# Residual stream in token-major layout, transposes by DMA crossbar, output weights resident: one core's attention and feed-forward block

## The chip, the cores and the metric

One core of a Trainium2 chip runs the whole program. The metric is device time in microseconds (us); a lower number is better. Runs of one kernel below agree within about 0.5%. All timed runs below are on one core, and each was interleaved with runs of the kernel before on the same chip. The experiments ran in three batches, each on another chip, and the kernel after did not run again beside them; the median of the kernel before moved by only 0.4 us between the batches (1413.09 to 1413.52), so times are compared across them, but differences of a few us are only good to about 2 us. "PE" is TensorE's matmul row in the profile, "PEld" its weight loads, "DVE" is VectorE, "ACT" is ScalarE, "POOL" is GpSimd and "SP" is SyncE, which here issues every DMA.

## The reference

An adaptive-layernorm block over 2048 tokens of width 1024: grouped-query attention over a cached window of 512 keys (32 query heads, 4 key heads, head size 128), then a gated feed-forward of width 3584. Cut to what matters:

```python
mod = (silu(c) @ w_mod).reshape(...)            # six rows of 1024: sa ca ga sb cb gb
h = layernorm(x) * (1 + ca) + sa
q = h @ wq                                      # 1024 -> 32 x 128
p = softmax(q @ k_window.T * 128 ** -0.5)       # 512 keys
x = x + ga * ((p @ v_window) @ wo)              # 4096 -> 1024
h = layernorm(x) * (1 + cb) + sb
x = x + gb * ((silu(h @ w_gate) * (h @ w_up)) @ w_down)
```

## The kernel before

Both kernels go through the tokens in four chunks of 512, first attention and output projection for all chunks, then the feed-forward for all chunks. A small tracker emits the instructions in program order and adds semaphore waits. Each engine's queue, and SP's queue of DMA issues, runs in order.

The kernel before keeps the residual feature-major (`xT`: feature on the partition, token along the free axis). So a layernorm sum runs over partitions and is a matmul with a matrix of ones; x has to be transposed on the way in and the result on the way out:

```python
def ln_task(...):                       # one chunk, dealt out as background steps
    for dt in range(DT):                # squares on GpSimd
        T.op(POOL, lambda: g.tensor_tensor(ln_sq[dt], xT[:, dt, chs], xT[:, dt, chs], ALU.mult), ...)
    for dt in range(DT):                # sums on TensorE
        mm(bank(bS), ones_bf, xT[:, dt, chs], ...)
    ...
    for dt in range(DT):
        mm(bank(bS), ones_bf, ln_sq[dt], ...)
    ...                                 # Ln and Exp on ScalarE for 1/sqrt, then three passes on VectorE
```

Per head, the attention output comes token-major out of the product with V, is normalised by VectorE, transposed by TensorE and copied out of PSUM:

```python
def otr(i):
    for j in range(TPC):
        transpose(bb[:, j * P:(j + 1) * P], o_s[os_][:, j, :], [B_os[os_]], PB[TRB])
    T.op(DVE, lambda: V.tensor_copy(oT_all[:, h, :], bb[:, 0:CH]), writes=[PB[TRB], B_oT[h]])

for i in range(NA + 3):                 # one turn per head; NA = 4 chunks x 32 heads
    if h % 4 == 2 and ...: load_wq(ch, h // 4 + 1)      # 1 MB of query weights
    if h == 8:  load_wo(0)                              # 2 MB of output weights, again in each chunk
    if h == 12: load_wo(1)
    ...
    qproj(i); scores(i - 1); pv(i - 2); otr(i - 3)
    ...                                 # after the last head of a chunk: oproj_plain(chunk)
```

The softmax here doesn't subtract the row's maximum and nothing guards it: scores larger than these inputs give would overflow.

## Time and profile before

The time is 1413.49 us (median of 3 runs, 1412.7 to 1415.42). The first lines come from the page of the kernel before: the span, the busy time of PE with its share and instruction count, the clock granted to TensorE in 40 slices of the span (9 is 90% or more), and the shares of the chain that ended last.

```profile
span 1412.8 us, 20538 instructions
PE 1346.9 (95%) x8445; PEld 700.7 (50%) x8592; DVE 610.2 (43%) x1324; ACT 415.0 (29%) x674; POOL 59.4 (4%) x65
...
PEclk7999999999999999999999999999999999999999
...
PE 91%; DVE 3%; issue 2%; ACT 2%; SPq 2%; DMA 1%; DVEq 0%; ACTq 0%
```

TensorE is the bound: it is busy 95% of the span, at nearly its full clock. What can be removed from it is in the groups of PE instructions by form (busy us, mean ns of one, idle time just before and its cause):

```profile
L289 PE MATMUL ps<-ident,arena 128*128 128x128 bf16 x528 | 51.0, 221 | 1.4 <-DVE arena L637 1.4
L285 PE MATMUL ps<-xT,ones_bf 128*128 128x512 bf16 x62 | 16.3, 410 | 4.0 <-DVE arena L637 3.0 <-DVE xT L355 0.9
L285 PE MATMUL ps<-ln_sq,ones_bf 128*128 128x512 bf16 x60 | 14.4, 379 | 4.2 <-DVE arena L637 3.2 <-DVE ln_mean L432 0.9
...
L289 PE MATMUL ps<-ident,xT 128*128 128x128 bf16 x128 | 10.5, 220 | 4.3 <-DVE xT L776 2.9 <-DVE xnat L789 1.4
```

The first line is the transposes of the attention output (512, and 16 of the keys), the next two are the layernorm sums, the last is the transposes of the result. A steady head in the timeline (start us, duration us, what) shows the pace:

```profile
326.70 0.38 PE L289 MATMUL ps<-ident,arena 128*128 128x128 bf16 x4
...
327.14 1.67 PE L285 MATMUL ps<-hT,arena 128*128 128x512 bf16 x7
...
328.65 1.96 PE L285 MATMUL ps<-arena 128*128 128x512 bf16 x20
...
330.45 0.38 PE L289 MATMUL ps<-ident,arena 128*128 128x128 bf16 x4
```

From one group of four transposes to the next it is 330.45 - 326.70 = 3.75 us. The durations overlap (327.14 + 1.67 lies after 328.65), because the profile models the ends of matmuls; so the pace is read from the starts.

### The profile page before, as it was taken

Reading aid. Unit: us, or ns where it says so; the run is one execution under the profiler, and the core shown is the slowest. Engines: PE = TensorE matmul, PEld = TensorE weight load, DVE = VectorE, ACT = ScalarE, POOL = GpSimd, SP = SyncE. Lnnn points to the kernel's source line nnn. Section 1 sums busy time; section 2 is a strip of 40 time slices with the busy share of each in tenths; the row PEclk is TensorE's granted clock in tenths of the full one; section 3 lists DMA queues with packets and bytes.
Section 4 is the critical chain, followed back from the end, with each engine's and each line's share of the span. In section 5 each row is a group of like instructions: output and inputs, shape, how many; then the busy total and the mean of one; then the engine's idle time right before and its main releaser. Section 6 shows DMA issues by size and latency. Waiting matters only on the chain.

```text
span 1412.8 us, 20538 instructions
## 1 busy us (share of the span) xinstructions
PE 1346.9 (95%) x8445; PEld 700.7 (50%) x8592; DVE 610.2 (43%) x1324; ACT 415.0 (29%) x674; POOL 59.4 (4%) x65
## 2 busy tenths in 40 slices
PE   5989999999999999999999999999999999999998
PEld 3556644556545566455554444444443444444443
DVE  4566554656613566235671245313331333124311
ACT  4455540456503666025760021001110111001100
POOL 0220021000010000110001100000000000000000
PEclk7999999999999999999999999999999999999999
DMA  9663204522143421434204485308721683129410
GB/s 304 199 183 120 90 31 120 154 86 61 61 120 111 120 69 61 117 92 121 75 16 114 141 268 171 111 15 271 222 96 52 200 278 126 52 94 300 151 52 30
DMA packets 237357, 178.53 MB, mean 126 GB/s; under 512 B 7888, under 2 KB 233168, under 8 KB 237264
## 3 DMA queue, kind: packets, MB, share of 16 engines
q1 hardware_dynamic: 237264, 177.22, 41.0%
q8 instruction: 67, 1.10, 0.3%
q14 instruction: 26, 0.21, 0.1%
HBM read 173.02 MB, written 4.19 MB: 125 GB/s over the span
## 4 chain that ended last, share of the span: by engine, by line
PE 91%; DVE 3%; issue 2%; ACT 2%; SPq 2%; DMA 1%; DVEq 0%; ACTq 0%
PE ps L285 89%; PE ps L289 2%; ACT arena L603 1%; DVE xT L776 1%; DMA xnat<-in_A_x_dram 1%; DVE arena L626 1%; DVE rl L623 1%; SPq L526 0%; SPq L361 0%; ACT L603 0%; ACT L447 0%; DVE xnat L789 0%; SPq L530 0%; DVE ln_var L440 0%; DVE arena L628 0%
## 5 line engine op out<-in xcount | busy, mean ns | idle before, releaser
L285 PE MATMUL ps<-arena 128*128 128x512 bf16 (+1 forms) x4431 | 671.0, 306 | 17.4 <-DVE xT L776 11.0
L285 PE MATMUL ps<-hT,arena 128*128 128x512 bf16 x2724 | 618.6, 380 | 16.0 <-ACT hT L466 6.4
L285 PEld LDWEIGHTS ps<-arena 128*128 128x128 bf16 x4480 | 365.8, 98 | 339.3 <-issue 15.3
L285 PEld LDWEIGHTS ps<-hT,arena 128*128 128x128 bf16 x2816 | 270.5, 98 | 318.5 <-DMA arena<-in_A_wq_dram 6.3
L603 ACT ACTIVATE arena<-ps 128x512 bf16<-128x512 f32 x512 | 305.5, 597 | 347.0 <-PE ps L285 312.2
L756 ACT ACTIVATE arena<-ps 128x512 bf16<-128x512 f32 x112 | 66.9, 597 | 543.7 <-PE ps L285 543.7
L757 DVE SCALAR_TENSOR_TENSOR arena<-arena,ps 128x512 bf16<-128x512 bf16 x112 | 77.0, 688 | 173.5 <-ACT arena L756 173.5
L591 DVE CAST arena<-ps 128x512 bf16<-128x512 f32 x128 | 88.4, 690 | 49.8 <-PE ps L285 45.1
L776 DVE SCALAR_TENSOR_TENSOR xT<-ps,c,xT 128x512 bf16<-128x512 f32 x32 | 22.6, 747 | 183.2 <-PE ps L285 183.2
L760 DVE SCALAR_TENSOR_TENSOR arena<-arena,ps 128x512 bf16<-128x512 bf16 x112 | 77.0, 688 | 53.8 <-PE ps L285 53.7
L651 DVE SCALAR_TENSOR_TENSOR xT<-ps,c,xT 128x512 bf16<-128x512 f32 x32 | 24.0, 751 | 152.3 <-PE ps L285 152.1
L427 POOL TENSOR_TENSOR ln_sq<-xT 128x512 bf16<-128x512 bf16 x56 | 58.4, 1060 | 717.3 <-PE ps L285 671.8
L626 DVE TENSOR_TENSOR arena<-ps,rl 128x384 bf16<-128x384 f32 x128 | 71.4, 558 | 4.4
L622 DVE RECIPROCAL rl<-ps 128x3 f32<-128x3 f32 x128 | 23.1, 180 | 110.7 <-PE ps L285 110.7
L637 DVE COPY arena<-ps 128x512 bf16<-128x512 bf16 x128 | 53.1, 415 | 0.2 <-PE ps L289 0.2
L289 PE MATMUL ps<-ident,arena 128*128 128x128 bf16 x528 | 51.0, 221 | 1.4 <-DVE arena L637 1.4
L628 DVE TENSOR_SCALAR arena<-ps,rl 128x128 bf16<-128x128 f32 x128 | 44.9, 351 | 4.6
L289 PEld LDWEIGHTS ps<-ident,arena 128*128 128x128 bf16 x528 | 35.7, 98 | 1.6 <-DVE arena L637 1.6
L462 DVE TENSOR_TENSOR ln_n<-ln_t,ln_B 128x512 bf16<-128x512 bf16 x64 | 28.4, 444 | 1.2
L459 DVE TENSOR_TENSOR ln_t<-xT,ln_A 128x512 bf16<-128x512 bf16 x64 | 27.5, 430 | 0.0
L623 DVE RECIPROCAL rl<-ps 128x1 f32<-128x1 f32 x128 | 21.5, 168 | 13.6 <-PE ps L289 0.5
L285 PE MATMUL ps<-xT,ones_bf 128*128 128x512 bf16 x62 | 16.3, 410 | 4.0 <-DVE arena L637 3.0
(48 smaller groups left out, 207.6 us busy)
## 6 DMA issues: line engine op xcount, KB each, us to landing
arena<-in_A_wq_dram SPq DMA_DIRECT2D x32, 1024.0 KB, 5.4
arena<-in_A_wo_dram SPq DMA_DIRECT2D x16, 2048.0 KB, 10.7
arena<-in_B_w_gate_dram SPq DMA_DIRECT2D x28, 1024.0 KB, 5.2
arena<-in_B_w_up_dram SPq DMA_DIRECT2D x28, 1024.0 KB, 7.2
arena<-in_B_w_down_dram SPq DMA_DIRECT2D x16, 1792.0 KB, 11.8
hT<-in_w_mod_dram SPq DMA_DIRECT2D x8, 1024.0 KB, 9.4
xnat<-in_A_x_dram SPq DMA_DIRECT2D x16, 256.0 KB, 5.6
arena<-in_w_mod_dram SPq DMA_DIRECT2D x4, 1024.0 KB, 10.2
```

Of the source, the lines that this page charges most:

```text
L285: T.op(PE, lambda: TE.matmul(out_ap, lhsT, rhs, start=start, stop=stop), reads=reads, writes=[bank_buf])
L289: T.op(PE, lambda: TE.transpose(out_ap, in_ap, ident[:, :]), reads=reads + [B_ident], writes=[bank_buf])
L427: T.op(POOL, lambda: g.tensor_tensor(ln_sq[dt][:, :], xT[:, dt, chs], xT[:, dt, chs], ALU.mult), reads=[B_xT[dt][ch]], writes=[B_sq[dt]])
L591: T.op(DVE, lambda: V.tensor_copy(qT_s[qs], bank(QB)), writes=[PB[QB], B_qT[qs]])
L603: T.op(ACT, lambda: A.activation(ex_s[es][:, kt, :], bank(b), AF.Exp, scale=att_scale), writes=[PB[b], B_ex[es]])
L626: T.op(DVE, lambda: V.tensor_tensor(o_s[os_][:, 0:3, :], in3, rl3, ALU.mult), reads=[B_rl], writes=[PB[OA], B_os[os_]])
L628: T.op(DVE, lambda: V.tensor_scalar(o_s[os_][:, 3, :], bank(OBT, P, 0), rl[:, 3:4], None, op0=ALU.mult), reads=[B_rl], writes=[PB[OBT], B_ ...
L637: T.op(DVE, lambda: V.tensor_copy(oT_all[:, h, :], bb[:, 0:CH]), writes=[PB[TRB], B_oT[h]])
L756: T.op(ACT, lambda: A.activation(th_s[ts_], bank(gb), AF.Tanh, scale=0.5), writes=[PB[gb], B_th[ts_]])
L757: T.op(DVE, lambda: V.scalar_tensor_tensor(out=t1_s[ts_], in0=th_s[ts_], scalar=1.0, in1=bank(gb), op0=ALU.add, op1=ALU.mult), reads=[B_th ...
L760: T.op(DVE, lambda: V.scalar_tensor_tensor(out=guT[:, ft, :], in0=t1_s[ts_], scalar=0.5, in1=bank(ub), op0=ALU.mult, op1=ALU.mult), reads= ...
L776: T.op(DVE, lambda: V.scalar_tensor_tensor(out=xT[:, dtile, chs], in0=bank(DNB[dcol]), scalar=c6[:, 5 * DT + dtile:5 * DT + dtile + 1], in ...
```

## The change

The intent is to take work that is not a large matmul off TensorE. The residual stays token-major (`x_res`: token on the partition). Layernorm sums become `bn_stats` on VectorE along the free axis. Layernorm outputs (128x1024 per tile, except in the first chunk) and attention outputs (128x512 per head) are transposed by DMA, SBUF to SBUF. The output projection and the down projection now have the token block as stationary operand and 512 weight columns as moving one, so their results come out token-major and no transpose is needed at the end; the two gates, now along the free axis, are spread to all partitions by 16 small matmuls. The output weights (8 MB) and the down weights (7 MB) are loaded once and stay. The exponential takes two PSUM banks at a time, and Silu replaces the tanh form. The core of the diff, with cuts:

```diff
-                for dt in range(DT):
-                    mm(bank(bS), ones_bf[:, :], xT[:, dt, chs], ...)
+                for hf in range(2):
+                    T.op(DVE, lambda: V.bn_stats(st_[sl][:, hf * 6:hf * 6 + 6], x_res[:, t, hf * 512:hf * 512 + 512]), ...)
+                T.op(DVE, lambda: V.bn_aggr(mv[sl], st_[sl]), ...)
+                T.op(POOL, ...)      # rstd = (var + eps) ** -0.5, two steps
+                T.op(DVE, lambda: V.tensor_scalar(nsc[sl], x_res[:, t, :], mean, rstd, subtract, mult), ...)
+                T.op(Q_ln[sl], lambda: SP.dma_start_transpose(dst[:, :, tt * P:(tt + 1) * P], nsc[sl]), ...)
...
-                for j in range(TPC):
-                    transpose(bb[:, j * P:(j + 1) * P], o_s[os_][:, j, :], [B_os[os_]], PB[TRB])
-                T.op(DVE, lambda: V.tensor_copy(oT_all[:, h, :], bb[:, 0:CH]), writes=[PB[TRB], B_oT[h]])
+                T.op(Q_tr[os_], lambda: SP.dma_start_transpose(oT_all[:, h, :]..., o_s[os_]...),
+                     reads=[B_os[os_]], writes=[B_oT[h]])
...
-                    if h % 4 == 2 and not (ch == 0 and h == 2):
-                        load_wq(ch, h // 4 + 1)
-                    if h == min(8, Hq - 2):
-                        load_wo(0)                       # in every chunk, 2 MB each
+                    if h % 4 == 1 and i > 4:
+                        load_wq(i // 4 + 1)
+                    if LATE0 <= i < LATE0 + DT:          # heads 2 to 9 of chunk 0, 1 MB each
+                        load_wml(i - LATE0)
+                    if LATE0 + 6 + DT <= i < LATE0 + 6 + 2 * DT:
+                        load_wo(i - (LATE0 + 6 + DT))    # heads 16 to 23 of chunk 0 only, 1 MB each
+                            row_bcast(0, 2 * DT)         # in one block, after the last modulation matmul
+                            row_bcast(1, 5 * DT)
...
-                    mm(bank(ob), wo_s[sl][:, h, dcol * P:(dcol + 1) * P], oT_all[:, h, :], ...)
+                        mm(bank(b), oT_all[:, h, j * P:(j + 1) * P], wo_s[:, h, hf * 512:(hf + 1) * 512], ...)
```

## The prediction

> **What bounds the kernel now.** TensorE. The busy table gives PE 1346.9 of 1412.8 us (95%) at a mean granted clock of 0.993 (cores view), and 91% of the chain that ended last is PE. By stage (windows view): start-up 28.3 us; attention of the four chunks 169.7, 131.0, 126.7 and 118.5 us; output projections about 55 us each; feed-forward chunks 155.9, 152.3, 152.3 and 155.4 us. In a steady head (timeline at 325 to 331 us) PE repeats every 3.74 us: twelve 512-column and sixteen 129-column matmuls in 3.52 us, then four 128x128 transposes in about 0.22 us. ACT needs 2.66 us and DVE about 3 us of it, so neither binds. Chunk 0 is different: 5.3 us a head, because x-tile transposes, late modulation, layernorm and their DMAs share it.
>
> **What goes away.** By the groups view: 512 attention-output transposes, about 50 us busy on PE (paced 0.22 us a head = 28 us); 128 layernorm sum matmuls, 31 us; 96 of the 128 x-tile transposes and all 128 output transposes, 8 + 10 us with about 8 us of waits before them. Also the Ln/Exp table loads (1.28 us each) that hold up exponentials, 11 us of PE waits on the down-projection residual (waits view), and about 46 MB of repeated output and down-weight loads.
>
> **What stays or comes.** The large matmuls are the same count, 5248 of 512 columns (about 0.2155 us each) and 2048 of 129 columns (0.0585 us): 1131 + 120 = 1251 us. Added: per head one DMA transpose of 128x512, 28 DMA transposes of 128x1024 for layernorm, 16 small broadcast matmuls. The exponentials become two of 1024 columns; with 0.597 us for 512 columns I estimate 2.05 us a head. DVE falls to about 1.6 us a head plus about 12 us of layernorm a chunk. Residual adds become two DVE passes, 1.4 us, under 6 to 7 us of PE work.
>
> **Sum.** Start-up 23 us (bounded by about 6 MB at the 300 GB/s of the first slice); attention 128 x 3.53 = 452; modulation and row broadcasts 13; DMA back-pressure in chunk 0 about 20 (8 MB of late modulation weights and 8 MB of output weights within some 20 heads, over 300 GB/s); projections 4 x 55; feed-forward 4 x 145.5 = 582; turns between stages and tail 15. **1325 us**, 6% faster. Nearly all of the gain is PE time on the critical path; some 35 to 45 us of it is chunk 0.
>
> **The DMA transposes are the doubt.** No trace here has one. The Trainium skill (DMA: Bandwidth & Descriptors, "Latency and other measured facts") gives 261 GB/s effective for a DMA transpose in one kernel; at that rate 128 KB takes an estimated 0.5 us, and the 3.5 us pace of a head would hide it. All DMAs go through SP's in-order queue, though, and output buffers are two deep: a transpose landing over about 6 us after its data is ready stops DVE's normalisation, then PE. A 1 MB load ahead of it lands in 5.4 us (DMA view), so margins are thin, and in chunk 0 absent.
>
> **Right if the profile shows** PE busy near 1270 us, no waits of DVE or PE for the transposes after chunk 0, about 3.5 us per head, chunk 0 near 145 us, feed-forward near 146 us, far fewer GB moved in later projections. **Wrong if** a 128x512 transpose occupies SP or the queues for over 3.5 us (attention then runs at the transposes' pace, and the time may exceed 1413), if they slow the weight loads beside them so qproj or gate/up wait, or if DVE waits for the small Pool power steps stretch start-up.
>
> Predicted 1325 us, 8 in 10 between 1290 and 1395; faster by over 2% 0.80, within 2% 0.09, slower by over 2% 0.11.

## The result, and the profile after

The kernel after takes 1327.35 us (median of 4 runs, 1325.78 to 1329.68). The ratio to the kernel before is 0.9388, with a 95% interval of 0.9375 to 0.9401. Ratios here are the mean time of one kernel's runs over that of the other's in the same rounds, so they are not quite the ratio of the medians. The output is correct, as in every run below.

The same lines from the page of the kernel after:

```profile
span 1324.0 us, 17825 instructions
PE 1271.1 (96%) x7602; PEld 649.8 (49%) x7744; DVE 455.6 (34%) x850; ACT 332.7 (25%) x372; POOL 26.2 (2%) x73
...
PEclk9989999999999999999999999999999999999999
...
PE 91%; DMA 5%; DVE 3%; issue 1%; POOL 0%; ACT 0%; SPq 0%; DVEq 0%
```

PE is busy 75.8 us less, and the span is 88.8 us shorter; so 13 us of the gain is time in which PE waited. The DMA in the chain is nearly all transposes: five of them in chunk 0 (41 us) and four in chunks 1 to 3 (17 us, beside which PE went on working). A steady head in the timeline:

```profile
308.65 0.18 DVE L510 RECIPROCAL rl<-ps 128x4 f32<-128x4 f32 x1 [1.11 <-PE ps L257]
308.87 0.69 DVE L513 TENSOR_TENSOR arena<-ps,rl 128x512 bf16<-128x512 f32 x1
309.59 4.71 SPq L516 DMA_TRANSPOSE arena<-arena  x2
...
312.18 0.18 DVE L510 RECIPROCAL rl<-ps 128x4 f32<-128x4 f32 x1 [1.11 <-PE ps L257]
```

The pace is now 312.18 - 308.65 = 3.53 us. The SP line merges two transposes, each issued as soon as VectorE has normalised a head. PE has no transposes between heads.

To see where the time went I cut both profiles at the VectorE residual additions, which read PSUM at the end of each output tile group, and so stand in both kernels. (The attention stages in the prediction were cut by eye at other points and are up to 5 us off; these are not.)

| stretch, us | before | after | difference |
|---|---|---|---|
| start to first residual (start-up, attention of chunk 0, one group of the projection) | 205.1 | 184.8 | -20.3 |
| last residual to next first one, chunks 1, 2, 3 | 133.3, 133.2, 128.6 | 121.2, 121.8, 118.9 | -33.2 |
| inside the four output projections | 196.8 | 193.4 | -3.4 |
| four feed-forward chunks, to their last residual | 609.6 | 580.2 | -29.4 |
| after the last residual | 6.2 | 3.8 | -2.4 |

Three things stand out. Start-up is not shorter: the first attention matmul is at 29.1 us (28.3 before). Attention of chunk 0 costs 184.8 - 29.1 = 155.7 us on this cut, while chunks 1 to 3 cost about 121, so chunk 0 still takes about 35 us more (a part of it is the late modulation, which only this chunk has). And outside chunk 0 the attention transposes hardly show. These are the waits of VectorE and PE between 25 and 190 us (total, times, longest):

```profile
DVE arena L513 <- DMA arena<-arena: 16.8, 8, 5.1
...
PE ps L257 <- DVE diag L448: 5.6, 8, 1.7
PE ps L257 <- DVE arena L513: 5.1, 5, 2.7
...
PE ps L257 <- DVE arena L471: 3.4, 1, 3.4
```

L513 is the normalisation of a head; it waits for a buffer that a transpose still reads. L448 builds the small operands that spread the gates. In chunks 1 to 3 (185 to 790 us) the first of these waits does not occur at all; VectorE waits 4.6 us there for layernorm transposes, and PE 0.4 us for a transpose. The time from issue to landing of the attention transposes shows why; first from 29 to 185 us (chunk 0), then from 250 to 680 us:

```profile
DMA to landing us min/median/max: 2.4/4.5/13.1
```

```profile
DMA to landing us min/median/max: 2.4/2.5/6.1
```

With two buffers, a transpose may take up to about two heads less the normalisation, some 6 us. In later chunks all stay within that (6.1 us at most); in chunk 0 not all do.

The feed-forward stages gain 29.4 us with no attention in them. The windows view of these stretches, before and after (stretch, length, busy time and count on PE, PEld, DVE, ACT, POOL, granted clock, DMA share, GB/s):

```profile
797.05:1406.65 609.60, 592.38 (x2751) 269.27 (x2804) 195.72 (x298) 70.67 (x116) 1.04 (x1) 1.00 0.45 143
```

```profile
740.08:1320.24 580.16, 577.33 (x2635) 262.84 (x2686) 150.97 (x248) 66.86 (x112) 9.46 (x24) 1.00 0.39 120
```

PE works 15.1 us less. The other 14.4 us is idle time of PE that is gone: before, it waited 14.2 us for VectorE's residual additions and copies of the result (L776, L789); after, no such wait is left.

### The profile page after: what moved, and what is told of

Read it like the earlier page. It is cut to its first block, busy times and chain, and to the rows that moved or that the text cites. A ratio compares the mean times of both kernels' runs of the same rounds, so it can differ in the third digit from the quotient of the medians.

```text
span 1324.0 us, 17825 instructions
## 1 busy us (share of the span) xinstructions
PE 1271.1 (96%) x7602; PEld 649.8 (49%) x7744; DVE 455.6 (34%) x850; ACT 332.7 (25%) x372; POOL 26.2 (2%) x73
## 4 chain that ended last, share of the span: by engine, by line
PE 91%; DMA 5%; DVE 3%; issue 1%; POOL 0%; ACT 0%; SPq 0%; DVEq 0%
PE ps L257 91%; DMA arena<-arena 3%; DMA arena<-nsc 1%; DVE st L362 0%; PE ps L261 0%; DVE arena L513 0%; DVE arena L471 0%; DMA h2s<-nsc 0%; DVE tmp L531 0%; DMA x_res<-in_A_x_dram 0%; DVE nsc L371 0%; DVE arena L376 0%; POOL rstd L368 0%; DVE arena L406 0%; DVE rowb L451 0%
## 5 line engine op out<-in xcount | busy, mean ns | idle before, releaser
L257 PE MATMUL ps<-arena 128*128 128x512 bf16 (+1 forms) x6276 | 1060.9, 328 | 23.7 <-DVE arena L513 6.2
L257 PEld LDWEIGHTS ps<-arena 128*128 128x128 bf16 x6400 | 546.2, 98 | 536.9 <-issue 9.2
L495 ACT ACTIVATE arena<-ps 128x1024 bf16<-128x1024 f32 x256 | 261.8, 1023 | 396.2 <-PE ps L257 384.5
L665 ACT ACTIVATE arena<-ps 128x512 bf16<-128x512 f32 x112 | 66.9, 597 | 519.5 <-PE ps L257 516.6
L257 PE MATMUL ps<-h2s,arena 128*128 128x512 bf16 x878 | 192.6, 379 | 0.9
L666 DVE TENSOR_TENSOR arena<-ps,arena 128x512 bf16<-128x512 f32 x112 | 77.5, 692 | 276.0 <-PE ps L257 276.0
L531 DVE TENSOR_TENSOR tmp<-ps,rowb 128x512 f32<-128x512 f32 x64 | 44.3, 692 | 328.9 <-PE ps L257 328.9
L257 PEld LDWEIGHTS ps<-h2s,arena 128*128 128x128 bf16 x896 | 87.7, 98 | 105.7
L471 DVE CAST arena<-ps 128x512 bf16<-128x512 f32 x128 | 88.5, 691 | 74.4 <-PE ps L257 74.4
L513 DVE TENSOR_TENSOR arena<-ps,rl 128x512 bf16<-128x512 f32 x128 | 88.5, 691 | 21.3 <-DMA arena<-arena 16.8
L362 DVE BATCH_NORM_STATS2 st<-x_res 128x6 f32<-128x512 bf16 x64 | 43.8, 684 | 3.7 <-DMA x_res<-in_A_x_dram 3.5
```

The lines of the kernel that those rows point to most:

```text
L257: T.op(PE, lambda: TE.matmul(out_ap, lhsT, rhs, start=start, stop=stop, skip_group_check=skip), reads=reads, writes=[bank_buf])
L362: T.op(DVE, lambda: V.bn_stats(st_[sl][:, hf * 6:hf * 6 + 6], x_res[:, t, hf * 512:hf * 512 + 512]), reads=[B_x[t]], writes=[B_st[sl]])
L471: T.op(DVE, lambda: V.tensor_copy(qT_s[qs], bank(QB)), writes=[PB[QB], B_qT[qs]])
L495: T.op(ACT, lambda: A.activation(ex_s[es][:, 2 * kp:2 * kp + 2, :], banks2(SCB + 2 * kp), AF.Exp, scale=att_scale), writes=[PB[SCB + 2 * k ...
L513: T.op(DVE, lambda: V.tensor_tensor(o_s[os_].rearrange("p (a b) d -> p a b d", a=2), psap(PVB * 512, [[512, 2], [130, 2], [1, P]]), rlb, A ...
L531: T.op(DVE, lambda: V.tensor_tensor(tmp[s][:, :], bank(b), rowb[ri][:, hf * 512:(hf + 1) * 512], ALU.mult), reads=[B_row[ri]], writes=[PB[ ...
```

## The experiments

Twelve kernels ran, three timed rounds each. "Gap 1, 2, 3" is the second row of the table, for chunks 1, 2, 3; "first residual" its first row.

### 1. The attention transposes back on TensorE, chunks 1 to 3 (pe_otr)

```diff
-                T.op(Q_tr[os_], ... dma_start_transpose ...)
+                if i < Hq:
+                    T.op(Q_tr[os_], ... dma_start_transpose ...)     # chunk 0 as it was
+            def otr(i): ...           # 4 transposes on PE and a copy on VectorE, one head later
```

> The changed kernel with the attention-output transposes of chunks 1 to 3 back on TensorE (chunk 0 still by DMA). Theory (the gain is PE time that was on the critical path, and the DMA transposes are hidden outside chunk 0): each of 96 heads gets 0.22 us longer, 3.52 to 3.74 us, so attention of chunks 1 to 3 goes from 114.2, 114.9 and 112.0 us to about 121, 122 and 119 us and the kernel to about 1346 to 1350 us. Rival (the transposes on PE hide in other waits and the gain came from elsewhere): these stages stay within 2 us each and the time at about 1327 us. Chunk 0 should stay at 149 us in both.

Measured: 1353.31 us, ratio 0.9581 (0.9565 to 0.9597). The gaps are 129.7, 129.7 and 126.8 us, that is 8.5, 7.9 and 7.9 us longer. The PE timeline of this kernel shows the old pace of 3.74 us (247.80 - 244.06):

```profile
243.84 0.38 PE L261 MATMUL ps<-ident,arena 128*128 128x128 bf16 x4
244.06 3.69 PE L257 MATMUL ps<-arena 128*128 128x512 bf16 x28
247.58 0.38 PE L261 MATMUL ps<-ident,arena 128*128 128x128 bf16 x4
247.80 3.69 PE L257 MATMUL ps<-arena 128*128 128x512 bf16 x28
```

The theory holds: 0.22 us for each of 32 heads is 7.0 us a chunk, and the last transpose of a chunk, which here stands before the projection, may add the other 1 us. So the DMA transposes give 24.3 of the 33.2 us gained in these gaps. The total is a little above the expected range; chunk 0, which has the same code, happened to be 2.9 us longer.

### 2. Four output buffers (os4)

```diff
-            NQT = 3; NEX = 2; NOS = 2
+            NQT = 3; NEX = 2; NOS = 4
```

> The changed kernel with four output buffers before the DMA transpose in place of two. Theory (chunk 0 loses about 20 us because the normalisation on VectorE waits for a buffer whose transpose stands behind 1 MB loads): the 16.8 us of VectorE waits for the transposes in chunk 0 mostly go, and chunk 0 goes from 149 to about 130 to 137 us, the kernel to about 1310 to 1316 us. Rival (chunk 0 is bound by the bytes it loads, not by the buffers): the wait only moves to the weight loads, and chunk 0 stays above 145 us. Later chunks unchanged in both.

Measured: 1326.79 us, ratio 0.939 (0.9376 to 0.9404); no gain. First residual at 185.9 us. The theory falls: the waits for the buffer are gone, as it said, but others took their place. Waits between 25 and 190 us:

```profile
DVE arena L376 <- DMA arena<-nsc: 7.0, 1, 7.0
...
PE ps L257 <- DVE arena L471: 5.8, 1, 5.8
...
PE ps L257 <- DMA arena<-in_A_wq_dram: 2.5, 1, 2.5
```

VectorE now waits for the layernorm transpose of the next chunk (`nsc`), and because its queue is in order, the copy of the query projection (L471) and then PE wait behind it. PE also waits for query weights. More buffers do not make late data earlier.

### 3. The loads of chunk 0 spread out (spread)

```diff
-                    if LATE0 <= i < LATE0 + DT:                  # heads 2, 3, 4, ... 9
+                    if i in WML_AT:                              # heads 2, 3, 5, 6, 8, 9, 11, 12
...
-                    if LATE0 + 6 + DT <= i < LATE0 + 6 + 2 * DT: # heads 16, 17, ... 23
+                    if 18 <= i <= 32 and i % 2 == 0:             # heads 18, 20, ... 32
...                                                               # x chunks 2, 3: heads 15, 17, not 3, 6
```

> The changed kernel, two output buffers as before, with the same loads of chunk 0 spread out: late modulation weights at two in three heads, output weights at every second head up to the end of the chunk, x chunks later. Theory (bursts of 1 MB loads at one per head exceed the 300 GB/s that the queues show, and the transposes wait in line behind them): most of the 16.8 us of VectorE waits go, and chunk 0 falls from 149 to about 130 to 138 us. Rival (the issue of transposes on the SP queue itself, 1.2 us and up to 4.2 us each, is what costs): the waits stay, chunk 0 above 145 us.

Measured: 1317.17 us, ratio 0.9323 (0.9307 to 0.9338); first residual at 175.9 us, 8.9 us earlier. By the definition used in the expectation, chunk 0 falls from 148.8 to about 140 us, a little short of the range. VectorE's waits for the transposes fall from 16.8 to 7.8 us. The SP queue issues as many transposes as before, so their issue cost is not what hurt; the rate of loads beside them is. Part of the remaining excess has another cause, which experiment 5 shows.

### 4. Start-up interleaved (start_pipe)

```diff
-            for t in range(TPC):
-                ...stats, Pool power, normalise, transposes, copy of tile t
+            stats0(0)
+            for t in range(TPC):
+                if t + 1 < TPC: stats0(t + 1)     # statistics of the next tile first
+                ...normalise and transpose tile t; copy of tile t - 1
```

> The changed kernel with the start-up of the first four token tiles interleaved: the statistics of the next tile go to VectorE before the normalisation of this one, so the Pool step is hidden, and the copy out of PSUM comes one tile later. Theory (start-up is bound by the serial chain VectorE, Pool, VectorE, PE, VectorE of 5.0 us per tile): the first attention matmul comes at about 22 to 24 us in place of 29.1 us and the kernel gains 5 to 7 us. Rival (start-up is bound by the modulation weights' DMA, 6 MB at 305 GB/s): the first attention matmul stays within 1.5 us of 29.1 us.

Measured: 1321.07 us, ratio 0.9347 (0.9333 to 0.936). The first attention matmul, in the kernel after and then in this one:

```profile
29.10 3.00 PE L257 MATMUL ps<-arena 128*128 128x512 bf16 x7 [2.68 <-DVE arena L376]
```

```profile
20.80 3.57 PE L257 MATMUL ps<-arena 128*128 128x512 bf16 x8 [2.31 <-DVE arena L376]
```

The theory holds: start-up was bound by the chain of VectorE, Pool, VectorE, PE and VectorE (5.0 us a tile), not by the DMA. Of the 8.3 us, 6.3 stay in the time; in the profiles, chunk 0 gives back about 2.5 us; that it reaches its loads sooner is a likely reason, not a tested one.

### 5. The gate rows dealt out (row_spread)

```diff
-                            row_bcast(0, 2 * DT)
-                            row_bcast(1, 5 * DT)
+                            ROW_AT = i            # from here: 2 operands per head on VectorE,
+                                                  # their 2 matmuls in the next head, for 8 heads
```

> The changed kernel with the 16 small matmuls that spread the two gate rows over all partitions dealt out, two per head over eight heads, in place of one block in which PE waits for VectorE 8 times. Theory (the block costs its own 7.5 us and, because PE is mostly idle in it, a granted clock of about 0.5 for some 8 us after its start): chunk 0 falls by 7 to 11 us from 149 us, the kernel to about 1316 to 1320 us, and no stretch of granted clock near 0.5 is left at 88 to 97 us. Rival (the block only fills time in which chunk 0 would wait for its loads anyway): under 3 us gained.

Measured: 1317.65 us, ratio 0.9323 (0.9307 to 0.9338), 9.7 us less than the kernel after (7.5 us between the two profiled runs). The windows view of that kernel (columns as above), and then of this one:

```profile
85.00:90.00 5.00, 1.83 (x27) 1.08 (x24) 4.05 (x15) 0.39 (x1) 0.00 (x0) 0.98 0.75 115
90.00:95.00 5.00, 2.36 (x11) 1.23 (x12) 3.31 (x11) 0.00 (x0) 0.00 (x0) 0.50 0.57 192
95.00:100.00 5.00, 5.00 (x32) 2.62 (x31) 1.72 (x4) 2.05 (x2) 0.00 (x0) 0.84 0.00 0
```

```profile
85.00:90.00 5.00, 5.00 (x71) 3.40 (x70) 3.96 (x11) 2.72 (x3) 0.00 (x0) 1.00 0.81 92
90.00:95.00 5.00, 5.00 (x46) 3.11 (x44) 3.07 (x8) 3.32 (x4) 0.00 (x0) 1.00 0.95 247
```

From the last matmul before the block (it ends at 85.5 us) to the next large one (94.7 us) PE was idle 5.8 of 9.2 us, with no single idle time over 1.7 us; the granted clock was 0.50 from 89.8 to 96.6 us, so still low after PE was busy again. So 5.6 us in the list of waits stood for some 8 to 10 us of time. The Trainium skill, "TensorE: Matmul & The Clock Gate", section "Why this matters for your kernels", warns of idle gaps of more than about 3 us between bursts of matmuls, and its section "A second HAM failure mode: psum-queue depth-cycling" says that frequent short idle times can slow the clock too. This trace agrees with the second: no gap was over 1.7 us, and PE was busy 1.18 of the 3.4 us before the clock fell (86.4 to 89.8 us).

Waits for transposes cost clock as well. The same trace of the kernel after has two more such stretches, 69.3 to 72.7 and 130.8 to 137.6 us at 0.50, after PE had been busy 0.73 and 1.55 of 3.4 us while VectorE stood behind a transpose. No run isolates what they cost.

### 6. Every attention transpose twice (tr_twice)

```diff
+                T.op(Q_dup[os_], lambda: SP.dma_start_transpose(dup[os_]..., o_s[os_]...),   # into scratch
+                     reads=[B_os[os_]], writes=[B_dup[os_]])
```

> The changed kernel with every attention-output transpose issued twice, the second copy into a scratch buffer that nobody reads. Theory (outside chunk 0 the transposes are hidden and there is room: one takes 1.2 us of the SP queue and lands in 2.6 us, a head lasts 3.52 us): attention of chunks 1 to 3 stays within 2 us of 114.2, 114.9 and 112.0 us, and only chunk 0 (149 us) grows. Rival (the transposes run at the edge of what hides): chunks 1 to 3 grow by over 5 us each.

Measured: 1361.16 us, ratio 0.9633 (0.9618 to 0.9647). The gaps grow by 6.9, 4.4 and 3.7 us, first residual by 20.5 us. In chunks 1 to 3 VectorE now waits for transposes, 11.4 us in total (253 to 776 us):

```profile
DVE arena L516 <- DMA arena<-arena: 11.4, 11, 1.7
DVE arena L376 <- DMA arena<-nsc: 8.3, 2, 4.4
```

Neither theory is right in full. The transposes are hidden with one per head, but the room is less than one more per head. How the added time splits between the SP queue and the DMA engines this run doesn't tell.

### 7. Output weights loaded again in each chunk (wo_reload)

```diff
+                    if ch > 0 and 16 <= h < 24:
+                        load_wo(h - 16)            # the same 8 MB, 1 MB per head
```

> The changed kernel with the output weights loaded again in chunks 1 to 3, 1 MB per head in heads 16 to 23, same buffers, same bytes. Theory (a burst of one 1 MB load per head makes the transposes wait in line, as in chunk 0): attention of chunks 1 to 3 grows by 4 to 10 us each, the kernel by 12 to 30 us, and the VectorE waits for the transposes show up there. Rival (keeping the output weights resident saves only bytes that were hidden): each chunk within 1.5 us, the kernel within 4 us of 1327 us.

Measured: 1347.05 us, ratio 0.9535 (0.9519 to 0.9552). The gaps are 126.5, 127.2 and 126.4 us: 5.3, 5.4 and 7.5 us longer. The waits of chunk 0 turn up in chunks 1 to 3 (235 to 761 us), where the kernel after has none of the first kind and 4.6 us of the second:

```profile
DVE arena L513 <- DMA arena<-arena: 13.5, 9, 2.6
DVE arena L376 <- DMA arena<-nsc: 9.2, 2, 4.6
```

The theory holds. Keeping the output weights resident is worth about 20 us against this schedule of reloads, because the reloads make the transposes land late. Whether they do so on SP's queue or on the DMA engines this run doesn't tell (experiment 9 speaks for the engines). A reload spread over more heads was not tried.

### 8. Layernorm transposes on TensorE (ln_pe)

```diff
-                    T.op(Q_ln[sl], lambda: SP.dma_start_transpose(dst[...], nsc[sl]), ...)
+                    for dt in range(DT):
+                        transpose(bank_bf(XB)[:, dt * P:(dt + 1) * P], nsc[sl][:, dt * P:(dt + 1) * P], ...)
+                    T.op(DVE, lambda: V.tensor_copy(dst[...], bank_bf(XB)...), ...)
...                                                 # chunk 1's layernorm starts at head 15 instead of 4,
...                                                 # with two background steps per head in chunk 0, not one
```

> The changed kernel with the layernorm transposes of the 28 later tiles on TensorE with a copy on VectorE, in place of the DMA transposes of 128x1024. Theory (PE time is what counts): 8 transposes at about 0.055 us each, 0.44 us a tile, 28 tiles, 12 us more, so about 1336 to 1343 us; feed-forward chunks 1 to 3 of 145.0 us become about 146.8 us in their first three and attention of chunks 1 to 3 about 116 us. Rival (the DMA transposes of layernorm, which are issued for 2 to 4 us each, do harm in chunk 0 that outweighs this): the kernel stays at or below 1328 us, with chunk 0 below 145 us.

Measured: 1332.91 us, ratio 0.943 (0.9414 to 0.9446), 5.6 us more than the kernel after. The gaps grow by 1.3, 0.7 and 1.1 us, the first three feed-forward chunks by 1.8 us each (102.7 to 104.5 us up to their first residual), and the first residual is 1.1 us earlier. So the layernorm transposes by DMA do bring PE time, but less than I expected: the feed-forward chunks grew as expected, the attention gaps by about half of it, and chunk 0, where the transposes of chunk 1's layernorm fall, not at all. In chunk 0 the layernorm was also moved, so for that chunk the run does not separate the two.

### 9. The loads from another queue (act_loads)

```diff
-            Q_wml = [dq("q_wml%d" % k) for k in range(DT)]
+            Q_wml = [dq("q_wml%d" % k, nc.scalar) for k in range(DT)]
...                # likewise output weights, query weights and x of the attention loop: A.dma_start for SP.dma_start
```

> The changed kernel, its loads at the same heads as before, but the weight and x loads of the attention loop issued from ScalarE's queue, so the transposes alone are on SyncE's. Theory (a transpose stands in line behind whole loads of its own queue): the median landing of a transpose in chunk 0 falls, VectorE waits for transposes there fall from 16.8 to under 5 us, chunk 0 from 149 to about 138 to 143 us. Rival (all queues share the same 16 engines and chunk 0's bursts fill them, whoever issues): waits stay over 10 us and chunk 0 within 4 us of 149 us, or worse where a full queue holds up ScalarE's exponentials.

Measured: 1350.45 us, ratio 0.9558 (0.9538 to 0.9578); first residual at 209.7 us, 24.9 us later. The gaps, where the loads are few, are 0.4 to 1.1 us shorter. First the wait of VectorE for attention transposes between 20 and 205 us, then the landing of the transposes issued from 29 to 178 us (4.7 us median for the kernel after in the same stretch):

```profile
DVE arena L517 <- DMA arena<-arena: 34.6, 8, 7.9
```

```profile
DMA to landing us min/median/max: 2.4/7.1/15.3
```

The theory of a line within one queue falls; the rival stands, and it was worse than no gain. The Trainium skill, "DMA: Bandwidth & Descriptors", section "Issuing engines are not separate DMA queues", says that DMAs of all issuing engines run on the same 16 DMA engines and interleave. This run agrees: a queue of its own didn't shield the transposes. ScalarE waited only for PE and, once, for the key cache (18.5 us; 19.2 in the kernel after), so a hold-up of its exponentials is not the reason. Why the transposes land even later than before was not tested; SP no longer holds back the loads while a transpose waits for its data, which would let the loads run further ahead, but that is an argument only.

### 10. One part alone, in the kernel before (before_dma_otr)

```diff
                     reads=[B_rl], writes=[PB[OBT], B_os[os_]])
+                T.op(Q_tr[os_], lambda: SP.dma_start_transpose(oT_all[:, h, :]..., o_s[os_]...), ...)
...
-                for j in range(TPC): transpose(...)          # otr() is empty now
```

> The kernel before with one part of the change alone: the attention-output transposes by DMA in place of TensorE, everything else as it was (output weights not resident, 2 MB loads). Theory (0.22 us of PE per head is on the critical path): the attention stages of 131.0, 126.7 and 118.5 us fall by about 7 us each less some waits behind the 2 MB loads, the kernel goes from 1413 to about 1388 to 1396 us. Rival (the 2 MB weight loads in front of the transposes eat the gain): above 1406 us, with VectorE waits for the transposes of over 15 us.

Measured: 1461.16 us, ratio 1.0342 (1.0326 to 1.0359). The part that gave 24 us above costs 48 us here. Neither theory named the reason. PE's longest waits are for loads, not for transposes:

```profile
PE ps L285 <- DMA arena<-in_A_wq_dram: 29.5, 22, 6.4
PE ps L289 <- DMA xnat<-in_A_x_dram: 27.6, 6, 9.9
```

The timeline shows how one comes about:

```profile
362.55 4.72 SPq L631 DMA_TRANSPOSE arena<-arena  x2
...
365.70 0.35 DVE L629 TENSOR_SCALAR arena<-ps,rl 128x128 bf16<-128x128 f32 x1
...
367.36 0.53 SPq L540 DMA_DIRECT2D arena<-in_A_wq_dram  x1
...
373.68 1.68 PE L285 MATMUL ps<-hT,arena 128*128 128x512 bf16 x7 [1.82 <-DMA arena<-in_A_wq_dram]
```

The second transpose waits for VectorE (365.70 + 0.35 us). The load of query weights stands behind it in SP's in-order queue, goes out at 367.36 us and takes 5.7 us (median), so PE waits 1.82 us. The longest waits of SP's own queue during attention, first in the kernel before (29 to 740 us), then in this one (29 to 800 us), show what changed:

```profile
SPq L79 <- PE ps L285: 614.7, 36, 33.3
```

```profile
SPq L631 <- DVE arena L592: 269.5, 67, 12.4
```

In the kernel before, SP waits only for PE, that is, for a buffer to be read out; so it runs ahead of the program and issues a load as soon as its buffer is free. Here it follows VectorE head by head.

### 11. The same with loads issued earlier (before_dma_early)

```diff
-                    if h % 4 == 2 and not (ch == 0 and h == 2):
+                    if h % 4 == 1 and not (ch == 0 and h == 1):        # query weights one head earlier
...
-                    if 1 <= i <= len(XT_REST): transpose_x_tile(XT_REST[i - 1])
+                    if 3 <= i <= len(XT_REST) + 2: transpose_x_tile(XT_REST[i - 3])   # x used 2 heads later
```

> The kernel before with attention-output transposes by DMA, as in the earlier run of 1461 us, but query-weight loads issued one head earlier and x tiles loaded two heads earlier. Theory (the earlier run lost because loads stand in SyncE's in-order queue behind a transpose that waits for VectorE, so they reach PE late: 29.5 us of waits for query weights, 27.6 us for x tiles): both waits fall under 10 us, and the time falls to about 1395 to 1420 us. Rival (the transposes slow the transfers themselves): the waits stay over 20 us in total and the time over 1440 us.

Measured: 1412.4 us, ratio 0.9994 (0.9978 to 1.0009). (Using an x tile two heads later is the same lead as loading it two heads earlier.) The two waits fall from 57.1 to 11.2 us:

```profile
PE ps L285 <- DMA arena<-in_A_wq_dram: 6.5, 3, 4.5
PE ps L289 <- DMA xnat<-in_A_x_dram: 4.7, 1, 4.7
```

The cause is shown: 49 us came from loads held up in SP's queue, with what these waits brought along (the granted clock was 0.976 in the profiled run of experiment 10 and is 0.985 here). And still the DMA transposes bring nothing to the kernel before. Its gaps are 138.3, 136.1 and 123.8 us, so chunk 3, which has less layernorm work beside it, gains 4.8 us and chunks 1 and 2 lose 5.0 and 2.9 us. VectorE waits 18.5 us for transposes in the whole run, with 2 MB loads of output weights in each chunk; that those loads are the cause here is likely from experiment 7 but was not tested in this kernel. The kernel after issues its query weights at `h % 4 == 1`, with no reloads: the DMA transposes pay off in the kernel that has those two parts of the change, and not alone; which other parts they need was not tested.

### 12. The gains together (best_os4)

The edit is the sum of experiments 2, 3, 4 and 5.

> The changed kernel with the spread loads, the interleaved start-up, the gate rows dealt out over eight heads and four output buffers, together. If the gains are separate (9 us for the loads, 6 for the start-up, 8 for the rows): about 1302 us, chunk 0 near 130 us after a start of 21 us. If they overlap, because an earlier start or fewer stalls only reach the same loads sooner: 1306 to 1312 us.

Measured: 1298.05 us (1297.0 to 1299.16), ratio 0.9185 (0.9171 to 0.9198); this beats both kernels. The first residual is at 157.5 us (184.8 in the kernel after), the gaps are as before. From its page:

```profile
span 1296.7 us, 17957 instructions
PE 1272.2 (98%) x7744; PEld 648.2 (50%) x7744; DVE 454.5 (35%) x850; ACT 333.0 (26%) x372; POOL 26.8 (2%) x73
```

Alone, the four gave 0.6, 10.2, 6.3 and 9.7 us, in total 26.8; together they gave 29.3. So they at least add up. The deeper buffers may count for something once the loads are spread, and the granted clock is now 1.00 throughout (0.994 in the profile of the kernel after), though no run isolates either.

## Why the prediction was right

The prediction said 1325 us and the time is 1327.35. Point by point:

- **TensorE binds and its removed work is time saved: right.** PE busy was to be near 1270 us and is 1271.1. A steady head was to take about 3.5 us and takes 3.53. Experiment 1 shows the mechanism for the attention transposes by putting them back (24.3 us over three chunks), experiment 8 for the layernorm transposes (5.6 us). No run undid the rest of the gain; from the profiles alone, about half of the feed-forward's 29.4 us is PE work (15.1 us), and the other half is PE's waits for VectorE (14.4 us). The prediction had named 11 us of these waits, so "nearly all" PE time was a little too strong.
- **Stages: right, with errors that cancel.** A feed-forward chunk was to take near 146 us and takes 145.0; projections were 55 and are 55.3; chunk 0 was to be near 145 us and is 148.8, of which experiments 3 and 5 name about 10 us each (load bursts, gate rows). But "35 to 45 us" of the gain was to be in chunk 0, and its attention gained 21 us (176.8 to 155.7 us on the cut above); chunks 1 to 3 gained more together, 33.2 us. Data moved during the first three projections fell from about 77 to about 22 GB/s.
- **Start-up: wrong by 6 us.** The term was 23 us, from 6 MB at 300 GB/s, and it measured 29.1. The prediction named the Pool power steps as a risk but did not price the chain; experiment 4 shows it was that. Nor is 300 GB/s a ceiling: the queues moved 388 and 422 GB/s from 8 to 12 and 12 to 16 us of this start-up.
- **Turns and tail: too large.** The term was 15 us. The tail after the last residual is 3.8 us and the turns after projections cost PE 2.4 us in waits. This made up for the start-up (6 us over) and for attention with modulation and back-pressure (490 us on the prediction's cut, where its terms add up to 485). That the total came within 0.2% is therefore partly luck.
- **Modulation and rows at 13 us: too small for the rows.** The clock was left out of it: it fell to 0.50 in the block of small matmuls, and dealing the matmuls out saved 9.7 us.
- **The transposes are hidden after chunk 0: right, for a partly wrong reason.** From the Trainium skill's 261 GB/s ("DMA: Bandwidth & Descriptors", "Latency and other measured facts") I estimated 0.5 us per transpose. The trace shows 2.4 us at the least from issue to landing of 128 KB, of which SP's issue alone is 1.19 us. That figure of the page is a rate; the same section also speaks of a fixed cost of about 2 us per DMA, which I overlooked. How much of the 2.4 us is fixed no run separates: transposes of twice the size took 3.1 us at the least. The margin of about 6 us was right in size, and experiment 6 shows that twice the transposes do not fit.
- **Resident weights: under-priced.** The prediction counted them as bytes. Experiment 7 shows about 20 us for reloads in bursts, which make the transposes late.

## What to carry to other kernels

When a kernel is bound by TensorE, look at the loads before you move its transposes to DMA. Here the move paid in full only where the queue that issues the transposes held up no load that PE would soon miss, and where no burst of large loads ran beside them, on whichever queue. Issue loads a step earlier first, and keep weights resident where they fit. Look for the stage where such a change gains least: here it was the first chunk, and what helped was to spread the loads and the small matmuls, not to deepen buffers. A block of small dependent matmuls cost its waits and then the clock; dealt out among large ones it did not.

## What the Trainium skill lacked or had wrong

- "DMA: Bandwidth & Descriptors" gives a rate for DMA transposes and a fixed cost of about 2 us for a DMA, but for this chip by name neither issue cost nor landing time of a transpose of these sizes, and nothing on how far loads beside it delay it. Here a 128x512 bf16 transpose from SBUF to SBUF takes about 1.19 us of SP's queue and 2.4 us at least to land, 2.5 us median in a quiet stretch, 4.5 us median and up to 13.1 us in chunk 0 beside 1 MB loads; one of 128x1024 takes 1.26 us to issue and 3.8 us to land (medians).
- The same page's rule that issuing from several engines does not help bandwidth agrees with experiment 9, but it does not say that it can hurt small transfers that run beside the loads: the median landing of the transposes rose from 4.7 to 7.1 us and the kernel took 23 us more.
- No page that I read warns that a DMA issue that waits for a compute engine takes away SP's run-ahead for the loads behind it in program order; that cost 49 us in experiment 10, which experiment 11 got back.
- "TensorE: Matmul & The Clock Gate" names idle gaps over about 3 us, and frequent micro-idles without a size. A number for the second: with gaps of at most 1.7 us each and PE busy 1.18 of 3.4 us, the granted clock fell to 0.50.
